# A new order for the first 441 of 973 steps of a gated linear attention kernel

## The chip, the core and the metric

The kernel runs on one core of a Trainium2 chip. That core has five engines, each with a queue of its own that it works off strictly in order: PE (TensorE, matrix products), DVE (VectorE), ACT (ScalarE), POOL (GpSimd) and SP (SyncE, which here only issues DMAs). They wait for each other through semaphores. The metric is the device time of one execution in microseconds (us), as the median of several runs.

## What is computed

Eight batches of eight heads, 576 tokens, 64 channels per head: a linear attention with a softmax of q over its channels and of k over the tokens, and after it a value product gated by a causal convolution of 5 taps, and an output product.

```python
q_s = softmax(q, axis=-1)            # over 64 channels
k_s = softmax(k, axis=2)             # over 576 tokens
kv  = einsum('bhsd,bhde->...', k_s^T v)      # 64x64 per head
x   = einsum('bhsd,bhde->bhse', q_s, kv)     # -> (8, 576, 512)
gate = sigmoid(sum_k conv_w[k] * shift(x, 4 - k))
out  = (gate * (x @ w_val)) @ w_out
```

The weights come as 64-bit floats and are put together on the chip into 32-bit ones.

## The kernel before

The work is cut into named steps; `ORDER` lists 973 of them as text ("`kv 1`", "`q_sub 0 2 p`"), and the program runs the list from top to bottom under a manual schedule. A step issues one or a few instructions on one engine, so the list sets the order of every engine's queue. A last letter names the engine where there is a choice: `a` ACT, `v` DVE, `p` POOL. The first number is the batch, the second mostly the part: channels lie across partitions, in four blocks of 128 (`x 1 0` is block 0 of batch 1). `HOMES` gives each tile the buffer that it takes, one digit per tile in order of allocation; a tile must wait until all readers of the buffer's last tenant are through. The four letters of `bank` are pairs of PSUM banks.

The steps that matter here:

- weights, eight slabs of 512 columns (0 to 3 are w_val, 4 to 7 w_out): `load_words`, then `part` and `field`, `scaled`, `signed`, `joined` make one 32-bit slab, `w_high` and `w_low` split it for two exact passes (L276 to L327). `value b m` needs slab m, `project b n` slab 4 + n, high and low both.
- q: `q_max`, `q_sub`, `q_exp` or `q_each`, `q_sum`, `q_eps`, `q_rec`, `q_mul` on five parts of the tokens (the fifth, the tail, is shared by two batches); `q_turn` transposes on PE, `q_turned` copies out, `tail_turn` and `tail_turned` do so for the tail.
- k of batches 0 and 1: `k_top`, `k_raise`, `k_turn`, `k_turned`, `k_tail_turn`, `k_tail_turned`. For later batches `k_peak` takes maxima per column, which go through memory (`k_row`, `k_spread`).
- `kv` (80 matmuls), `kv_sums` and `kv_norm` give `kvd`; `attend b 0` and `attend b 1` make x of blocks 0, 1 and 2, 3 in PSUM.
- x: `x_high` and `x_low` split x out of PSUM, `first` and four `tap` steps make the gate's sum from the same PSUM bank, `sigmoid` ends it. For batch 0, blocks 0 and 1, the convolution runs on PE as `conv` instead, which takes the banks of `x 0 0` and `x 0 1` as soon as `x_low` has read them.
- `value` (24 matmuls of 128x288, the products with the low part of x last, in the order in which `x_low` ran), `gated`, `g_high`, `g_low`, `project` (24 matmuls), `copy`, `put`.

`attend 1 1` takes the PSUM banks of `x 1 0` and of a projection; it cannot start before all four taps on `x 1 0` are through.

Of the kernel before, what the change touches and what calls it, by code (L numbers as in the profile page):

```python
# [31 lines left out]
    load_words 3, field 3 v, scaled 3 v, signed 3, w_high 3 a, warm 12, load_q 0 2 5, load_kc 0 0, load_q 0 0 1,  # L32
    load_taps, load_q 0 1 2, load_ident, load_words 0, part 3 a, load_kc 0 1, load_kc 0 2, load_kc 0 3, load_words 1,
    q_max 0 2 3, q_sub 0 2 p, q_max 0 3 5, joined 3 v, q_exp 0 2 3, k_top 0 0, q_sub 0 3 p, q_each 0 4, q_exp 0 3 4,
    q_max 0 0 1, q_each 0 0, tap_field p, tap_scaled v, load_v 0, load_vt 0, load_km 2 2, tap_part v, tap_signed,
    q_max 0 1 2, tap_joined p, diag p, load_km 2 1, load_words 2, load_q 1 0 5, q_sub 0 1 p, k_raise 0 0, q_sum 0 2 5,
    q_eps 0 2 5 p, q_exp 0 1 2, k_top 0 1, k_raise 0 1, k_turn 0 0, q_rec 0 2 5, field 0 p, k_top 0 2, k_raise 0 2,
    q_mul 0 2 p, k_top 0 3, k_raise 0 3, q_sum 0 0 2, q_eps 0 0 2 v, q_mul 0 3 p, q_rec 0 0 2, k_turn 0 1,
    k_turned 0 1 v, k_turned 0 0 a, k_tail_turn 0, k_tail_turned 0 v, scaled 0 a, field 1 p, scaled 1 a, signed 1,
    q_mul 0 1 a, q_mul 0 4 p, tail_turn 0, conv_rows, q_mul 0 0 p, part 1 a, load_kc 1 1, tail_turned 0 a, joined 1 p,  # L40
    field 2 p, scaled 2 p, signed 0, w_high 0 a, kv 0, k_peak 2 2, tail_high 0 a, kv_sums 0, kv_norm 0 v, part 2 a,
    conv_kv, signed 2, q_turn 0 0, q_turned 0 0 a, part 0 a, load_words 4, load_km 2 0, joined 0 p, q_turn 0 1,
    q_turned 0 1 a, attend 0 0, w_low 3 p, x_high 0 1 a, q_max 1 0 2, q_sub 1 1 p, x_low 0 1, x_high 0 0 a, x_low 0 0,
    load_words 5, attend 0 1, w_high 1 a, q_max 1 2 4, joined 2 p, x_high 0 3 a, first 0 3 a, tap 0 3 2, tap 0 3 3,
    tap 0 3 0, x_low 0 3, w_low 1 p, tap 0 3 1, load_words 6, first 0 2 a, q_exp 1 1 2, x_high 0 2 a, w_high 2 p,
    part 5 a, q_each 1 2, w_low 0 p, x_low 0 2, q_each 1 3, q_sub 1 0 p, load_kc 1 3, load_kc 1 0, k_top 1 1,
    k_top 1 0, k_top 1 3, tap 0 2 0, conv, field 5 p, scaled 5 p, signed 5, joined 5 p, load_v 1, field 4 p,
    conv_gate 1, conv_gate 0, load_kc 1 2, value 0 1, value 0 0, q_sum 1 2 4, k_raise 1 0, q_exp 1 0 1, k_raise 1 3,
    sigmoid 0 3, gated 0 1, w_low 2 p, k_top 1 2, gated 0 0, k_raise 1 1, k_raise 1 2, q_sum 1 0 2, load_km 2 3,
    scaled 4 p, signed 4, q_eps 1 2 4 p, q_rec 1 2 4, k_turn 1 0, k_turned 1 0 a, load_q 2 0 5, g_high 0 1 a,  # L50
# [5 lines left out]
    load_km 3 3, q_turned 1 1 a, gated 0 3, g_high 0 3 a, g_low 0 2 v, k_peak 3 2, attend 1 0, first 1 1 a, field 6 p,
    first 1 0 a, scaled 6 p, signed 6, tap 1 1 2, g_low 0 3 p, load_km 5 3, project 0 0, tap 1 0 3, load_k 2,
    tap 1 0 1, load_km 5 0, part 6 a, q_sub 2 1 p, w_high 6 a, k_row 2, x_high 1 1 a, project 0 1, tap 1 0 2,
    load_q 3 0 5, tap 1 1 3, q_sub 2 2 p, x_high 1 0 a, x_low 1 0, tap 1 0 0, k_spread 2, copy 0 0 a a, put 0 0,
    part 7 a, copy 0 1 a a, load_km 3 1, attend 1 1, x_high 1 3 a, first 1 2 a, k_peak 3 3, joined 6 p, load_qc 3 1,  # L60
    tap 1 1 1, x_high 1 2 a, signed 7, w_high 7 a, w_low 6 p, q_sub 2 4 p, tap 1 1 0, sigmoid 1 1, joined 7 p,
    x_low 1 1, q_sub 2 0 p, x_low 1 3, x_low 1 2, k_peak 3 1, load_kt 2, load_km 3 0, project 0 2, w_low 7 p,
    value 1 0, copy 0 2 a a, load_vt 4, k_peak 3 0, q_max 3 0 4, q_sub 2 3 p, put 0 2, first 1 3 a, tap 1 2 1,
    load_km 4 1, sigmoid 1 0, gated 1 0, k_sub 2 0 p, k_sub 2 2 p, tap 1 2 3, load_km 4 3, k_sub 2 4 p, q_sub 3 0 p,
    load_v 2, q_exp 2 0 5, q_sum 2 0 5, project 0 3, copy 0 3 a a, far 1 2 2, k_sub 2 1 p, k_sub 2 3 p, g_high 1 0 a,
    g_low 1 0 p, q_eps 2 0 5 a, q_rec 2 0 5, q_mul 2 0 p, q_mul 2 3 p, k_exp 2, k_row 3, kt_exp 2, q_mul 2 2 p,
    load_v 4, load_km 6 1, k_peak 4 3, k_peak 4 1, tap 1 2 0, tap 1 3 2, value 1 3, put 0 1, tap 1 3 3, tap 1 3 0,
    tap 1 3 1, value 1 1, gated 1 1, near 1 2 2, kv 2, kv_sums 2, load_km 4 0, kv_norm 2 v, q_mul 2 1 a, q_mul 2 4 a,
    q_turn 2 0, sigmoid 1 3, gated 1 3, k_peak 5 0, k_peak 5 3, sigmoid 1 2, tail_turn 2, q_turned 2 0 a,
    tail_turned 2 a, load_qc 3 0, tail_high 2 a, q_sub 3 1 v, q_sub 3 3 p, k_peak 4 0, put 0 3, k_spread 3,  # L70
    q_sub 3 2 p, g_high 1 3 p, g_low 1 3 v, g_high 1 1 p, g_low 1 1 v, q_turn 2 1, q_turned 2 1 a, load_q 4 0 5,
    value 1 2, gated 1 2, q_exp 3 0 4, attend 2 0, far 2 1 0, x_high 2 1 a, g_high 1 2 v, g_low 1 2 p, project 1 3,
    far 2 1 3, first 2 1 a, q_total 3, tap 2 1 1, load_km 4 2, first 2 0 a, tap 2 0 2, copy 1 3 a a, near 2 1 3,
    x_low 2 1, load_qc 3 3, tap 2 0 1, tap 2 1 2, tap 2 0 3, load_v 3, load_km 5 1, project 1 0, put 1 3, q_log 3,
    k_peak 4 2, k_sub 3 3 p, l_turn 3, near 2 1 0, l_row 3, far 2 0 0, k_row 4, q_max 4 0 5, k_sub 3 1 p,
    copy 1 0 a a, k_sub 3 0 p, load_km 5 2, project 1 2, copy 1 2 a a, k_sub 3 4 p, attend 2 1, first 2 3 a,
    x_high 2 0 a, near 2 0 0, first 2 2 a, project 1 1, x_high 2 3 a, q_sub 4 0 p, x_low 2 0, x_high 2 2 a, tap 2 3 1,
    k_sub 3 2 p, kt_exp 3, put 1 0, q_sub 4 2 p, copy 1 1 a a, sigmoid 2 0, q_sub 4 1 p, q_sub 4 4 p, k_peak 5 1,
    tap 2 2 0, sigmoid 2 1, l_spread 3, x_low 2 2, x_low 2 3, q_sub 4 3 p, tap 2 3 0, k_peak 6 1, value 2 1,
    gated 2 1, g_high 2 1 p, tail_high 3 a, l_sub 3 0 p, load_km 6 2, tap 2 2 1, q_exp 4 0 5, load_k 4, load_kt 4,  # L80
    tap 2 3 3, tap 2 2 2, k_exp 3, k_peak 6 2, tap 2 3 2, k_spread 4, c_exp 3 0, value 2 0, load_qc 3 2, l_sub 3 3 p,
    g_low 2 1 p, sigmoid 2 3, gated 2 0, load_qc 4 1, value 2 3, q_total 4, c_exp 3 3, gated 2 3, kv 3, value 2 2,
    kv_sums 3, load_q 5 0 5, k_peak 5 2, tap 2 2 3, kv_norm 3 v, l_sub 3 1 p, q_log 4, c_exp 3 1, attend 3 0,
    load_km 6 3, g_high 2 0 a, sigmoid 2 2, g_high 2 3 p, g_low 2 3 p, first 3 1 a, l_turn 4, gated 2 2, first 3 0 v,
    load_vt 6, far 3 1 0, k_row 5, tap 3 0 3, g_low 2 0 p, tap 3 0 1, g_high 2 2 p, put 1 1, g_low 2 2 p, project 2 0,
    x_high 3 1 v, l_sub 3 2 p, load_km 6 0, project 2 1, load_qc 4 3, tap 3 1 2, x_low 3 1, k_sub 4 3 p, put 1 2,
    c_exp 3 2, k_sub 4 4 p, copy 2 0 a a, tap 3 1 1, tap 3 1 3, x_high 3 0 a, l_row 4, copy 2 1 a a, q_max 5 0 4,
    k_sub 4 1 p, put 2 0, far 3 0 0, attend 3 1, load_qc 5 1, first 3 3 a, k_sub 4 2 p, first 3 2 a, q_sub 5 1 p,
    k_peak 6 3, x_high 3 3 a, put 2 1, k_sub 4 0 p, project 2 2, tap 3 0 2, q_sub 5 2 p, load_qc 4 0, l_spread 4,
    x_high 3 2 a, x_low 3 0, k_exp 4, x_low 3 3, tap 3 2 3, k_peak 6 0, project 2 3, copy 2 2 a v, near 3 0 0,  # L90
# [707 lines left out]
```

## Time and profile before

| | |
|---|---|
| time, median of 3 runs | 286.7 us (286.58 to 286.75) |
| profiled execution | 286.8 us, of which the span from first to last instruction is 284.9 us |
| PE busy | 278.9 us (98%) in 2640 matmuls |
| DVE busy | 232.0 us (81%) |
| POOL busy | 202.0 us (71%) |
| ACT busy | 193.1 us (68%) |
| granted TensorE clock | 1.00 of 2.4 GHz in all 40 slices |

Busy times are averages over the span; the first third is fuller than the last. A row of PE spans from the start of a matmul to its modelled end, and consecutive matmuls overlap, so PE counts as busy also where it runs below its rate. A row of DVE or POOL includes what it waited for after its start. Spans on POOL are rough.

### The profile page before, as it was taken

The page shows a single profiled execution, that of the slowest core. Times are in us where ns is not written, and L with a number is a line of the kernel's source. Part 1 is how long each engine was busy: PE and PEld are TensorE (multiplying, and loading weights), DVE is VectorE, ACT ScalarE, POOL GpSimd, SP SyncE. Part 2 cuts the span into 40 slices and gives each one's busy share as a digit, 9 for nine tenths or more (in the row PEclk, how much of TensorE's full clock was granted, in tenths as well). Part 3 has the DMA queues.
Part 4 walks back from the last instruction along what each step waited for, and adds up shares of the span by engine and source line. Part 5 has one row for each costly group of instructions (what it writes and reads, how often), then busy time and mean ns, then how long its engine had stood idle before and what let it go on. Part 6 is the DMA issues. An engine that isn't in the chain of part 4 may idle for free.

```text
span 284.9 us, 6648 instructions
## 1 busy us (share of the span) xinstructions
PE 278.9 (98%) x2640; PEld 250.5 (88%) x2640; DVE 232.0 (81%) x334; ACT 193.1 (68%) x323; POOL 202.0 (71%) x185
## 2 busy tenths in 40 slices
...
GB/s 224 391 413 400 410 378 204 189 208 238 333 221 412 39 238 327 315 248 210 382 412 254 206 246 336 268 157 138 158 163 156 222 0 2 44 41 85 0 83 85
DMA packets 23463, 62.93 MB, mean 221 GB/s; under 512 B 3432, under 2 KB 3976, under 8 KB 20744
## 3 DMA queue, kind: packets, MB, share of 16 engines
...
HBM read 52.96 MB, written 9.54 MB: 219 GB/s over the span
## 4 chain that ended last, share of the span: by engine, by line
PE 82%; ACT 6%; DVE 5%; POOL 3%; DMA 2%; issue 1%; SPq 0%; POOLq 0%
PE out_a L629 36%; PE val L629 32%; PE kv L520 6%; PE x L579 6%; DMA q<-in_q_tail 2%; DVE gate L604 1%; ACT q L505 1%; ACT qT L197 1%; POOL q L507 1%; PE qTps L545 1%; DVE ktop L375 1%; DVE qm L414 1%; POOL q L419 1%; DVE x L599 1%; ACT gh L197 1%
## 5 line engine op out<-in xcount | busy, mean ns | idle before, releaser
L629 PE MATMUL val<-x,w_val_hi 128*128 128x288 f32 x512 | 88.9, 295 | 0.0
L604 DVE SCALAR_TENSOR_TENSOR gate<-x,cw,gate 128x575 f32<-128x575 f32 (+3 forms) x98 | 78.3, 809 | 5.1 <-ACT gate L592 1.8
L629 PEld LDWEIGHTS val<-x,w_val_hi 128*128 128x128 f32 x512 | 75.2, 188 | 0.0
L629 PE MATMUL val<-x,w_val_lo 128*128 128x288 f32 x256 | 56.0, 300 | 0.0
L629 PE MATMUL out_a<-gh,w_out_lo 128*128 128x288 f32 x248 | 54.6, 301 | 0.0
L629 PE MATMUL out_a<-gh,w_out_hi 128*128 128x288 f32 x248 | 53.2, 296 | 0.0
L696 POOL TENSOR_TENSOR gl<-g,gh 128x576 fp32r<-128x576 f32 x22 | 32.2, 1465 | 17.9 <-DVE gh L199 8.3
L629 PEld LDWEIGHTS out_a<-gh,w_out_lo 128*128 128x128 f32 x248 | 39.3, 188 | 5.7 <-ACT o L203 1.8
L629 PE MATMUL out_a<-gl,w_out_hi 128*128 128x288 f32 x248 | 43.0, 295 | 0.0
L629 PEld LDWEIGHTS val<-x,w_val_lo 128*128 128x128 f32 x256 | 40.8, 188 | 1.3 <-DVE g L688 0.4
L613 POOL TENSOR_TENSOR gate<-gate,far 128x572 f32<-128x572 f32 (+3 forms) x22 | 29.1, 1325 | 17.6 <-DVE gate L604 9.7
L629 PEld LDWEIGHTS out_a<-gh,w_out_hi 128*128 128x128 f32 x248 | 39.8, 188 | 0.0
L203 ACT ACTIVATE o<-out_a 128x576 f32<-128x576 f32 x27 | 17.6, 651 | 31.7 <-PE out_a L629 29.8
L419 POOL TENSOR_TENSOR q<-q,qm 128x512 f32<-128x512 f32 x31 | 32.5, 1064 | 7.1 <-DVE qm L414 7.1
L629 PEld LDWEIGHTS out_a<-gl,w_out_hi 128*128 128x128 f32 x248 | 36.5, 189 | 0.0
L688 DVE SCALAR_TENSOR_TENSOR g<-gate,val 128x576 f32<-128x576 f32 x32 | 24.0, 749 | 14.0 <-PE val L629 8.2
L489 POOL TENSOR_TENSOR qc<-qc,lb 128x576 f32<-128x576 f32 (+1 forms) x17 | 24.2, 1432 | 9.7 <-DMA lb<-lrow 6.4
L354 POOL TENSOR_TENSOR k<-k,kmax 128x512 f32<-128x512 f32 x23 | 30.0, 1323 | 0.2
L599 DVE TENSOR_TENSOR x<-x,x 128x576 fp32r<-128x576 f32 x32 | 23.1, 749 | 2.5 <-ACT x L197 2.3
L616 ACT ACTIVATE gate<-gate 128x576 f32<-128x576 f32 x30 | 20.0, 683 | 7.5 <-DVE gate L604 7.3
L609 ACT ACTIVATE far<-x,cw 128x572 f32<-128x572 f32 (+3 forms) x22 | 16.2, 738 | 12.0 <-PE x L579 4.7
L197 ACT CAST x<-x 128x576 fp32r<-128x576 f32 x27 | 17.0, 642 | 7.1 <-PE x L579 4.3
(114 smaller groups left out, 457.3 us busy)
## 6 DMA issues: line engine op xcount, KB each, us to landing
...
```

Of the source, the lines that this page charges most:

```text
L197: nc.scalar.copy(out=out, in_=in_)
L203: nc.scalar.mul(out, in_, factor)
L354: engine(e).tensor_sub(kk[r, cs], kk[r, cs], mx[r, cs])
L419: engine(e).tensor_tensor(qq, qq, m, op=ALU.add if b < 2 else ALU.subtract)
L489: engine(e).tensor_sub(t, t, T["lb", b][:, p])
L599: nc.vector.tensor_sub(xl, T["x", b, p], T["xh", b, p].bitcast(F32))
L604: nc.vector.scalar_tensor_tensor(out=a, in0=x, scalar=w, in1=a, op0=ALU.mult, op1=ALU.add)
L613: nc.gpsimd.tensor_add(a, a, T["far", b, p, j])
L616: nc.scalar.activation(T["gate", b, p], T["gate", b, p], AF.Tanh, scale=0.5)
L629: nc.tensor.matmul(ps[:, cs], a[:, kb, ms], z[:, cs], start=(i == 0), stop=(i == len(parts) - 1))
L688: nc.vector.scalar_tensor_tensor(out=T["g", b, m], in0=T["gate", b, m], scalar=1.0, in1=T["val", b, m], op0=ALU.add, op1=ALU.mult)
L696: engine(e).tensor_sub(T["gl", b, m], T["g", b, m], T["gh", b, m].bitcast(F32))
```

## The change

The first 441 steps stand in a new order; the last 532 are as before. The same 973 steps are run. Of the first 441, 25 have another engine letter: from POOL to DVE `q_sub 0 2`, `q_mul 0 2`, `q_mul 0 0`, `q_eps 0 2 5`, `field 2`, `k_sub 3 1`; from DVE to POOL `joined 3`, `tap_scaled`, `q_sub 3 1`, `g_low 1 1`, `g_high 1 2`; from ACT to POOL `scaled 0`, `w_high 1`, `g_high 0 0`, `part 4`, `w_high 7`; from POOL to ACT `scaled 5`, `scaled 6`, `q_eps 1 2 4`, `g_high 1 3`, `g_high 2 1`; from DVE to ACT `q_eps 0 0 2`, `k_tail_turned 0`; from ACT to DVE `q_turned 2 0` and half of `copy 0 3`. The digits of `HOMES` follow the order. On PE, `tail_turn 0` moves ahead of the second `k_turn` of batch 0, and `q_turn 1 0` ahead of `kv 1`; `k_tail_turn 1` moves behind `value 0 3`. Two lines of the table, and some of the buffers:

```diff
-    q_max 2 0 5, q_mul 1 1 a, load_k 3, field 7 p, scaled 7 a, gated 0 2, g_high 0 2 a, kv 1, kv_sums 1, q_mul 1 2 p,
-    q_mul 1 0 p, q_turn 1 0, load_vt 2, w_low 4 p, tail_high 1 a, q_turned 1 0 a, kv_norm 1 v, q_turn 1 1,
...
+    q_mul 1 1 a, tap 0 2 3, sigmoid 0 2, q_turn 1 0, k_peak 3 2, k_peak 3 3, load_k 3, g_low 0 0 p, w_high 4 a,
...
+    k_peak 2 0, kv 1, kv_sums 1, kv_norm 1 v, load_v 2, joined 4 p, w_low 4 p, scaled 6 a, q_turned 1 0 a, q_turn 1 1,
...
-    "gate": "0123450123230154021345021354201534201532",
...
-    "f": "0123456103541206354036430214016032451036502104236540",
+    "f": "0123456103540156342104306240164502316504152653204135",
...
+    "gate": "0123450312203542130542310524130254130251",
```

Lines of the changed kernel's functions are one higher than before (L414 is L415).

On DVE at the start, from the sum over q's parts 2 to 4 (`qs`) to the norm of `kv 0`. Before:

```order
L429 TENSOR_REDUCE qs_187<-q_116 128x16
L438 TENSOR_SCALAR qs_187<-qs_187 128x16
L442 RECIPROCAL qs_187<-qs_187 128x16
L199 COPY k_223<-kps_1_214 128x4x256
L199 COPY ktz_83<-ktps_226 64x512
L290 TENSOR_SCALAR e_233<-e_233 128x512
L291 SCALAR_TENSOR_TENSOR e_233<-words_135,e_233 128x512
L290 TENSOR_SCALAR e_203<-e_203 128x512
L291 SCALAR_TENSOR_TENSOR e_203<-words_125,e_203 128x512
L339 TENSOR_REDUCE kpk_312<-km_2_170 128x1
L529 TENSOR_SCALAR ks_316<-kv_271 128x4
L530 RECIPROCAL ks_316<-ks_316 128x4
```

Now:

```order
L508 TENSOR_TENSOR q_99<-q_99,qs_167 128x512
L430 TENSOR_REDUCE qs_167<-q_99 128x16
L200 COPY k_230<-kps_1_215 128x4x256
L443 RECIPROCAL qs_167<-qs_167 128x16
L291 TENSOR_SCALAR e_203<-e_203 128x512
L292 SCALAR_TENSOR_TENSOR e_203<-words_114,e_203 128x512
L508 TENSOR_TENSOR q_99<-q_99,qs_167 128x512
L291 TENSOR_SCALAR e_225<-e_225 128x512
L292 SCALAR_TENSOR_TENSOR e_225<-words_136,e_225 128x512
L282 TENSOR_SCALAR e_304<-words_165 128x512
L340 TENSOR_REDUCE kpk_315<-km_2_161 128x1
L530 TENSOR_SCALAR ks_319<-kv_259 128x4
```

Two products with `qs` (L508) and `field 2` (L282) have come in, `ktz` (`k_tail_turned`) and the small sum ahead of the second reciprocal have gone; the other small sum (L439) has come from POOL.

On POOL, from q's products of batch 0 to the low parts of w_val (`f` is a joined slab, `e` one on its way). Before:

```order
L507 TENSOR_TENSOR q_116<-q_116,qs_187 128x512 x2
L281 TENSOR_SCALAR e_233<-words_135 128x512
L507 TENSOR_TENSOR q_116<-q_116,qs_187 128x512 x2
L294 TENSOR_TENSOR f_258<-e_233,f_258 128x512
L281 TENSOR_SCALAR e_265<-words_181 128x512
L205 TENSOR_SCALAR e_265<-e_265 128x512
L294 TENSOR_TENSOR f_336<-e_203,f_336 128x512
L327 TENSOR_TENSOR w_val_lo<-f_127,w_val_hi 128x4x128
L419 TENSOR_TENSOR q_183<-q_183,qm_366 128x512
L294 TENSOR_TENSOR f_321<-e_265,f_321 128x512
L327 TENSOR_TENSOR w_val_lo<-f_258,w_val_hi 128x4x128
L199 CAST w_val_hi<-e_265 128x4x128
```

Now:

```order
L200 CAST w_val_hi<-e_225 128x4x128
L206 TENSOR_SCALAR e_304<-e_304 128x512
L295 TENSOR_TENSOR f_325<-e_304,f_325 128x512
L328 TENSOR_TENSOR w_val_lo<-f_97,w_val_hi 128x4x128
L200 CAST w_val_hi<-e_304 128x4x128
L295 TENSOR_TENSOR f_356<-e_203,f_356 128x512
L420 TENSOR_TENSOR q_189<-q_189,qm_354 128x512
L295 TENSOR_TENSOR f_245<-e_225,f_245 128x512
L328 TENSOR_TENSOR w_val_lo<-f_245,w_val_hi 128x4x128
L420 TENSOR_TENSOR q_189<-q_189,qm_354 128x512
L282 TENSOR_SCALAR e_507<-words_393 128x512
L206 TENSOR_SCALAR f_516<-words_243 128x512
```

Three of four products have gone or moved, two `w_high` (CAST) and one `scaled` stand in; `field` of slab 5 and `part` of slab 4 (`words_393`, `f_516`) now come ahead of the `w_low 0` that follows.

On DVE behind `kv 1` (`ks`, `kvd`: its norm), to the taps on `x 1 0` (`x_0` there). Before:

```order
L536 TENSOR_TENSOR kvd_761<-kv_700,ks_741 128x256
L688 SCALAR_TENSOR_TENSOR g_3_775<-gate_3_390,val_3_654 128x576
L696 TENSOR_TENSOR gl_2_779<-g_2_696,gh_2_698 128x576
L339 TENSOR_REDUCE kpk_781<-km_2_652 128x1
L290 TENSOR_SCALAR e_795<-e_795 128x512
L291 SCALAR_TENSOR_TENSOR e_795<-words_398,e_795 128x512
L604 SCALAR_TENSOR_TENSOR gate_1_793<-x_1_784,cw,gate_1_793 128x574
L604 SCALAR_TENSOR_TENSOR gate_0_797<-x_0_783,cw,gate_0_797 128x575
L604 SCALAR_TENSOR_TENSOR gate_0_797<-x_0_783,cw,gate_0_797 128x573
L604 SCALAR_TENSOR_TENSOR gate_0_797<-x_0_783,cw,gate_0_797 128x574
L604 SCALAR_TENSOR_TENSOR gate_1_793<-x_1_784,cw,gate_1_793 128x575
L599 TENSOR_TENSOR x_1_0_876<-x_0_783,x_1_0_876 128x576
```

Now:

```order
L537 TENSOR_TENSOR kvd_764<-kv_720,ks_761 128x256
L291 TENSOR_SCALAR e_526<-e_526 128x512
L292 SCALAR_TENSOR_TENSOR e_526<-words_395,e_526 128x512
L697 TENSOR_TENSOR gl_2_818<-g_2_709,gh_2_715 128x576
L340 TENSOR_REDUCE kpk_315<-km_3_713 128x1
L340 TENSOR_REDUCE kpk_315<-km_1_163 128x1
L605 SCALAR_TENSOR_TENSOR gate_0_804<-x_0_785,cw,gate_0_804 128x575
L605 SCALAR_TENSOR_TENSOR gate_0_804<-x_0_785,cw,gate_0_804 128x572
L600 TENSOR_TENSOR x_1_0_813<-x_0_785,x_1_0_813 128x576
L605 SCALAR_TENSOR_TENSOR gate_0_804<-x_0_785,cw,gate_0_804 128x573
L605 SCALAR_TENSOR_TENSOR gate_1_859<-x_1_786,cw,gate_1_859 128x573
L605 SCALAR_TENSOR_TENSOR gate_0_804<-x_0_785,cw,gate_0_804 128x574
```

`gated 0 3` (L688) stands ahead of `kv 1` now; `signed 6` comes right behind the norm and `g_low 0 2` (L697) behind it; there are two `k_peak` instead of one; one `x_low` stands ahead of the last taps on `x_0`.

## Rows read from the trace of the kernel before

**Rows 1.** Waits of PE over the span: who for whom, total us, times, longest.
```profile
PE qTtps L559 <- POOL q L507: 0.8, 1, 0.8
```

**Rows 2.** Rows of the tile `cv` (conv), 26 to 34 us: waits by releaser, us, times.
```profile
  DVE x L599: 1.1, 2
```

**Rows 3.** Timeline of PE at conv and before `attend 1 0`: start, length, [idle <- releaser].
```profile
27.14 5.73 PE L675 MATMUL cv<-qT,dg 64*64 64x288 f32 x80
...
52.79 1.20 PE L579 MATMUL x<-qT,kvd 64*64 64x288 f32 x16 [0.24 <-ACT qT L197]
```

**Rows 4.** The chain that ended last, from 60 us: start, us, what.
```profile
60.59 1.13 PE x L579 x16
61.72 3.39 PE out_a L629 x24
```

**Rows 5.** Stretches: length; busy of PE, PEld, DVE, ACT, POOL; clock, DMA share, GB/s.
```profile
11.00:28.00 17.00, 15.35 (x174) 9.09 (x176) 16.30 (x26) 16.62 (x38) 13.95 (x16) 1.00 1.03 410
...
61.00:69.00 8.00, 8.00 (x67) 7.50 (x60) 7.97 (x12) 6.53 (x10) 6.73 (x7) 1.00 0.73 239
```

**Rows 6.** Timeline of DVE, start stretch, and one product at 83 us.
```profile
4.45 0.43 DVE L281 TENSOR_SCALAR e<-words 128x512 f32<-128x512 f32 x1 [4.45 <-DMA words<-in_w_val]
...
16.63 0.70 DVE L438 TENSOR_SCALAR qs<-qs 128x16 f32<-128x16 f32 x1
...
18.61 0.67 DVE L199 COPY ktz<-ktps 64x512 f32<-64x512 f32 x1
...
26.33 1.42 DVE L599 TENSOR_TENSOR x<-x,x 128x576 fp32r<-128x576 f32 x2
...
83.75 0.68 DVE L419 TENSOR_TENSOR q<-q,qm 128x512 f32<-128x512 f32 x1
```

**Rows 7.** Timeline of POOL, 27 to 34 us.
```profile
27.41 1.05 POOL L419 TENSOR_TENSOR q<-q,qm 128x512 f32<-128x512 f32 x1
28.41 1.30 POOL L294 TENSOR_TENSOR f<-e,f 128x512 int32<-128x512 int32 x1
29.65 1.30 POOL L327 TENSOR_TENSOR w_val_lo<-f,w_val_hi 128x512 fp32r<-128x512 f32 x1
...
33.84 0.65 POOL L281 TENSOR_SCALAR e<-words 128x512 f32<-128x512 f32 x1
```

**Rows 8.** Timeline of ACT at `q_turned 0 0`.
```profile
23.26 1.01 ACT L197 COPY qT<-qTps 128x1024 f32<-128x1024 f32 x1 [0.31 <-PE qTps L545]
```

**Rows 9.** Timeline of DVE around `kv 1` and batch 1.
```profile
49.63 0.74 DVE L688 SCALAR_TENSOR_TENSOR g<-gate,val 128x576 f32<-128x576 f32 x1
...
51.11 0.42 DVE L536 TENSOR_TENSOR kvd<-kv,ks 128x256 f32<-128x256 f32 x1
...
54.03 0.69 DVE L291 SCALAR_TENSOR_TENSOR e<-words,e 128x512 int32<-128x512 int32 x1
...
59.55 0.81 DVE L604 SCALAR_TENSOR_TENSOR gate<-x,cw,gate 128x572 f32<-128x572 f32 x1
...
63.44 2.07 DVE L599 TENSOR_TENSOR x<-x,x 128x576 fp32r<-128x576 f32 x3
```

**Rows 10.** Timeline of ACT, 50 to 53 us.
```profile
50.34 0.61 ACT L203 ACTIVATE e<-e 128x512 f32<-128x512 f32 x1
50.86 0.67 ACT L197 CAST gh<-g 128x576 fp32r<-128x576 f32 x1
...
51.73 1.92 ACT L197 COPY qT<-qTps 128x1024 f32<-128x1024 f32 x2
```

**Rows 11.** Timeline of POOL and DVE where both read two tensors at once.
```profile
54.30 1.73 POOL L696 TENSOR_TENSOR gl<-g,gh 128x576 fp32r<-128x576 f32 x1 [0.82 <-ACT gh L197]
...
264.03 1.44 POOL L696 TENSOR_TENSOR gl<-g,gh 128x576 fp32r<-128x576 f32 x1
...
264.11 1.97 DVE L696 TENSOR_TENSOR gl<-g,gh 128x576 fp32r<-128x576 f32 x1 [0.77 <-POOL gh L199]
...
267.73 0.76 DVE L696 TENSOR_TENSOR gl<-g,gh 128x576 fp32r<-128x576 f32 x1 [0.77 <-POOL gh L199]
```

235 lines of the change are left out of this document (118 added, 117 removed).

## The prediction

> **What bounds the kernel now.** I read the page's busy shares first: TensorE has matmuls nearly throughout (table above), so time can only be won where it waits. Then the waits of TensorE, of which the longest is 0.8 us for the product of q's tail, `tail_turn 0` [rows 1]. The rows of matmuls overlap, so short stalls hide under "busy"; one tile's rows show them: the instructions of `conv` waited 1.1 us for DVE's `x_low` [rows 2], inside the stretch from 27.14 to 32.87 [rows 3]. The wait before `attend 1 0` is 0.24 [rows 3]. All of these lie before 53 us. From 53 us on the chain of waits is TensorE alone [rows 4]: after `attend 1 0` at 52.79 come two projections, `attend 1 1` at 60.59 and a third projection to 65.1. So a gain has to come from the first 53 us, some 2 to 3 us at the very most (0.8 + 1.1 + 0.24 and a little), and every microsecond that TensorE is made to wait later is paid in full. Last I read how full the others are: from 11 to 28 us DVE works 16.30 of 17 us, from 61 to 69 us 7.97 of 8 [rows 5]. DVE is nearly as full as TensorE, so which instruction stands on DVE decides.
>
> **The start, to conv.** The diff moves steps between engines; I count the DVE queue up to `x_low 0 0`, on which conv waits. On it: three elementwise steps of 128x512 (`q_sub 0 2`, `q_mul 0 2`, `q_mul 0 0`), 0.68 each by DVE's one row of that form, `field 2` 0.43, `q_eps 0 2 5` 0.2 to 0.7 [rows 6]. Off it: `joined 3` (of the same size, 0.68 too), `q_eps 0 0 2` 0.70, `k_tail_turned 0` 0.67 [rows 6], `tap_scaled` (a few columns, some 0.2). On: 2.04 + 0.43 + 0.2 = 2.67; off: 2.25; net +0.42. Of DVE's 0.7 idle between 11 and 28 us [rows 5] I let 0.3 absorb it, the rest being short gaps between an instruction and the next that reads its result. That leaves +0.15. Then DVE and POOL get in each other's way: the `q_eps` of 0.70 us touches 16 columns only [rows 6], so most of it is a wait. The four moved instructions that read SBUF now meet POOL's queue (`q_eps 0 2 5` against `q_sub 0 1`, `q_mul 0 2` against `q_mul 0 4`); I take 0.2 for them together, nothing at the least, 1.05 (one whole POOL product, [rows 7]) at the most. `x_low 0 0` ended at 27.75 (26.33 + 1.42, [rows 6]); conv later by **+0.35**, bounds +0.1 and +1.2.
>
> The other way to conv is ACT: `q_exp 0 1 2` comes some 0.5 later, because on DVE one `q_max` more, some 0.6, stands ahead of `tap_signed`, for which POOL's `diag` and `q_sub 0 1` wait. ACT's own list up to `q_turned 0 0` is about as long as before (`scaled 0` goes, `k_tail_turned 0` and a small `q_eps` come), and ACT idled 0.31 there for the transposes [rows 8]; with `tail_turned 0` no longer waiting behind `signed`, I take this way as level, 0 to +0.3 and not added to DVE's +0.35, since the later of the two counts. `tail_turn 0` itself moves ahead of the second `k_turn`: its 0.8 us wait goes [rows 1], but what follows waits for ACT and DVE instead, so I count nothing for it.
>
> **POOL, to value 0 0.** POOL now does `w_high 1`, `joined 2`, `w_low 3`, `w_high 2`, `joined 0`, `q_sub 1 1`, `joined 1`, `w_low 1`, `q_sub 1 0`, `field 5`, `part 4`, `w_low 0`. `joined 2` waits for `signed 2` on DVE, which I put at 24.8 (it ended at 25.08 before, and now stands one `conv_kv` earlier but behind the longer queue). From there, start to start: five of joined and w_low at 1.24, two q_sub at 1.0 and 1.15, three with one input (`w_high 2`, `field 5`, `part 4`) at 0.6 to 0.7 [rows 7], together 10.3, and w_low 0's own 1.30: done at 36.4 to 36.5. `w_low 1` lies 3.9 earlier, 32.6, and is needed when conv ends, 32.87 before and 33.2 now: covered by 0.6. `w_low 0` is needed one product of 24 matmuls (3.2 to 3.3) later, at 36.4 to 36.5: **+0.1**, bounds 0 and +0.5 (`part 4` has no POOL row of its form).
>
> **kv 1 late.** `q_turn 1 0` now runs ahead of `kv 1`, so ACT can move its result while `kv 1` runs: the wait of 0.24 before `attend 1 0` goes [rows 3]. One more change of form on TensorE costs some 0.05. **-0.2**.
>
> **After kv 1.** Here lies the price. `attend 1 1` takes the PSUM bank of `x 1 0` and so waits for the last tap on it. Before, `kvd` was done at 51.53 and `attend 1 0` came 1.26 later (52.79), `attend 1 1` 7.8 after that [rows 3, 4, 9]: DVE had 9.06 us from kvd and needed 8.83 (59.55 + 0.81 - 51.53) [rows 9]. Now `attend 1 0` follows kvd at once: DVE has 7.9. Its list up to that tap (now `tap 1 0 2`) loses `gated 0 3`, one tap and the 0.20 wait and gains one `k_peak`: about -0.67 - 0.75 - 0.2 - 0.1 + 0.66, or 7.75. Spare 0.15. Nor is there room further on: the last `x_low` of batch 1 ended at 65.51 [rows 9], and `value 1 0`, which began at 65.1 (61.72 + 3.39, [rows 4]), reads it in its last group, 2.9 later: 2.5 spare. Now 1.2 of that is gone with kvd, and two `k_peak` and `tap 1 3 1` come in for `gated 0 3`, +1.4: nothing left.
>
> Into that queue falls a collision. Straight behind kvd stand the two-input instruction of `signed 6` and `g_low 0 2`, both with two SBUF inputs. kvd now ends at 51.53 + 0.98 (one `q_turn` more ahead of it) + 0.45 = 52.96, so they start at about 53.4 and 54.1. POOL's next is `g_low 0 3`, waiting for ACT's `g_high 0 3`. `gated 0 2` (49.63 before, [rows 9]) comes at 49.4: +0.45 from above, one `k_peak` of 0.66 less ahead. Behind its end at 50.15 ACT does g_high, scaled 6, q_turned, part 6, g_high: 0.57 + 0.52 + 0.95 + 0.57 + 0.67 = 3.3 (start to start, the last its whole length) [rows 10], ending at 53.45. So POOL's g_low asks at 53.5, in the middle of `signed 6`, and ahead of DVE's g_low. What that does is in the trace: a POOL g_low that met `signed 6` took 1.73 instead of 1.44, and a DVE g_low that met a POOL g_low took 1.97 instead of 0.76 [rows 9, 11]. So DVE's g_low waits out POOL's, 1.3 to 1.4 us; less the spare of 0.15, `attend 1 1` is **+1.2** late, bounds 0 and +1.4. Once paid it isn't paid again at `value 1 0`, since TensorE is later too.
>
> These rows are what the Trainium skill, "SBUF — State Buffer", section "Who interferes with whom", states as a rule: a DVE instruction with two SBUF inputs contends with a GpSimd instruction that reads SBUF, and the one that comes second blocks until the first is done. By that rule all three products moved to DVE are new collisions too, each up to one POOL product: the sum would then reach +1.2 at conv instead of +0.35, and 289.1 in all. I keep the smaller value, since the count puts POOL idle beside `q_mul 0 0` and the DVE one first beside `q_sub 0 2`.
>
> **Sum.** The profiled execution took 286.8 us: the span of 284.9 and 1.9 around it; it lies 0.1 over the median of 286.7. 0.35 + 0.1 - 0.2 + 1.2 = +1.45: 288.25 against 286.8, 288.2 against the median, if nothing later than 83 us is late. There the last 532 steps keep their order, and TensorE passes on what it got.
>
> **Rivals.** (a) No collision: ACT brings `g_high 0 3` after 54.1 and DVE's g_low goes first; 0.6 us decides, which is about what my count may be off. Then +0.25, 287.0, and up to 0.4 more at `value 1 0`, where nothing is spare. (b) The start gets shorter and the time falls: if the instructions on DVE up to `x_low 0 0` come without the collisions and the new order saves its waits, conv starts when `attend 0 1` is through, up to 1.1 us earlier [rows 2]; with the 0.2 at kv 1 and no loss later that is 286.7 - 0.2 - (0.5 to 1.1) = 285.4 to 286.0. For it: POOL is relieved of three products and two small sums by then, and all waits of TensorE lie there. Against it: DVE, the engine that conv waited for, gets more. It decides once `x_low 0 0` ends before 27.4 instead of 27.75. (c) A further late place: `q_turned 2 0` and half of `copy 0 3` come to DVE before 86 us (some 1.6), and the last `g_low` of batch 1 goes through POOL behind three more; where that outlasts TensorE, another 0.8 to 1.0: 289.2. That the table is not followed is no rival: the order of instructions is written out.
>
> **How the numbers follow.** Forecast (collision) 0.45, at 287.5 to 288.8; (a) 0.25; (b) 0.20; (c) 0.10. A run of this kernel can tell some 0.2% (0.57 us) from no change: faster is under 286.1, slower over 287.3. Faster 0.20 is (b); within 0.2%, 0.25, is (a); slower, 0.55, the forecast and (c). The range leaves out about half of (b) and most of (c): 285.7 to 288.9. The cases have both signs, and the forecast's own range is 287.5 to 288.8.
>
> **What would show it.** In the changed kernel's profile: `conv` begins its steady run at 28.1 (27.8 before); `value 0 0` begins at 36.5; no wait for ACT before `attend 1 0`, at 53.0; a DVE `gl` of about 2 us near 54 with a POOL `gl` beside it; `attend 1 1` at 62.0 instead of 60.8, with a wait for a DVE tap. Wrong would be: `conv` at or before 27.5 (then (b)), a `gl` of 0.76 on DVE near 54 (then (a)), or a wait of TensorE after 83 us (then (c)).

## The result: 1.0% slower, and more than half of it where no loss was forecast

The changed kernel takes 289.4 us (median of 4 runs, 289.05 to 290.0) against 286.6 us before: a ratio of 1.0098 (95% interval 1.0086 to 1.011), 2.7 us slower. That is the forecast sign, but outside the range: 288.2 was forecast, 288.9 was its upper end. The profiled execution has a span of 287.8 us (284.9 before), at a granted clock of 1.00.

TensorE's waits over the span, by who was waited for. Columns: total us, times, longest. Before the change the longest, behind the warm-up, was the 0.8 us for POOL's product [rows 1], and none lay behind 53 us.

```profile
PE kps L387 <- ACT kc L380: 1.1, 1, 1.1
PE x L580 <- ACT qT L198: 1.0, 2, 0.8
...
PE x L580 <- DVE gate L605: 0.9, 1, 0.9
PE out_a L630 <- POOL gl L697: 0.6, 1, 0.6
PE val L630 <- ACT x L198: 0.3, 1, 0.3
...
PE val L630 <- POOL w_val_lo L328: 0.2, 1, 0.2
```

The first two lie ahead of `conv`; the other four are new. To see what each is worth I took the start of each of TensorE's steps from the two timelines (the last column is rounded after subtracting):

| step | before | changed | later by |
|---|---|---|---|
| `conv` | 27.14 | 27.18 | 0.04 |
| `value 0 0` | 36.10 | 36.55 | 0.44 |
| `q_turn 1 1` | 51.52 | 51.89 | 0.37 |
| `attend 1 0` | 52.79 | 52.98 | 0.19 |
| `attend 1 1` | 60.52 | 61.67 | 1.14 |
| `kv 2` | 77.84 | 79.04 | 1.19 |
| `attend 2 0` | 85.96 | 87.05 | 1.08 |
| `project 1 0`, behind `project 1 3` | 90.39 | 92.30 | 1.91 |
| `project 1 1`, behind `attend 2 1` | 98.02 | 100.35 | 2.34 |
| `value 2 0`, behind `value 2 1` | 104.58 | 107.46 | 2.88 |

From there to the end the distance stays at 2.88. So there are five losses: 0.40 at `value 0 0`, 0.95 at `attend 1 1`, and, behind 83 us, 0.83, 0.43 and 0.54. The first two are those of the forecast, the last three are not.

**At 53 us** DVE and POOL, from their timelines (start, length):

```profile
53.20 0.69 DVE L292 SCALAR_TENSOR_TENSOR e<-words,e 128x512 int32<-128x512 int32 x1
53.82 1.98 DVE L697 TENSOR_TENSOR gl<-g,gh 128x576 fp32r<-128x576 f32 x1
```

```profile
53.65 1.53 POOL L697 TENSOR_TENSOR gl<-g,gh 128x576 fp32r<-128x576 f32 x1 [1.21 <-ACT gh L198]
```

POOL's `g_low 0 3` starts 0.17 us ahead of DVE's `g_low 0 2`, and DVE's takes 1.98 us; in [rows 11] an undisturbed one took 0.76. This is the forecast collision, within 0.3 us of where it was put. Before the change DVE's product ran first, and POOL's came at 54.30 [rows 11]:

```profile
52.11 0.89 DVE L696 TENSOR_TENSOR gl<-g,gh 128x576 fp32r<-128x576 f32 x1
```

**At 87 us** the same happens a second time:

```profile
86.29 0.74 DVE L340 TENSOR_REDUCE kpk<-km 128x1 f32<-128x576 f32 x1
86.95 1.82 DVE L697 TENSOR_TENSOR gl<-g,gh 128x576 fp32r<-128x576 f32 x1
88.90 0.75 DVE L689 SCALAR_TENSOR_TENSOR g<-gate,val 128x576 f32<-128x576 f32 x1
```

```profile
86.74 1.42 POOL L697 TENSOR_TENSOR gl<-g,gh 128x576 fp32r<-128x576 f32 x1
89.72 0.66 POOL L200 CAST gh<-g 128x576 fp32r<-128x576 f32 x1 [1.56 <-DVE g L689]
90.47 1.42 POOL L697 TENSOR_TENSOR gl<-g,gh 128x576 fp32r<-128x576 f32 x1
```

```profile
91.94 0.53 PE L630 MATMUL out_a<-gl,w_out_hi 128*128 128x288 f32 x2 [0.56 <-POOL gl L697]
```

DVE's `g_low 1 3` (86.95) meets POOL's `g_low 1 1`, which was on DVE before the change. There the two ran on DVE one after the other, 0.7 us each, and POOL stood idle:

```profile
85.02 1.41 DVE L696 TENSOR_TENSOR gl<-g,gh 128x576 fp32r<-128x576 f32 x2
```

```profile
87.74 1.43 POOL L696 TENSOR_TENSOR gl<-g,gh 128x576 fp32r<-128x576 f32 x1 [3.88 <-DVE gh L199]
```

In the changed kernel, behind the collision, `gated 1 2` (88.90), `g_high 1 2` and `g_low 1 2` come late one after the other, and `project 1 3` waits for the last.

**At 96 to 106 us** the queue of ACT, from its timeline:

```profile
96.66 1.28 ACT L617 ACT_TABLE_LOAD   x1
97.95 0.69 ACT L617 ACTIVATE gate<-gate 128x576 f32<-128x576 f32 x1
98.54 0.63 ACT L204 ACTIVATE o<-out_a 128x576 f32<-128x576 f32 x1
...
102.66 0.74 ACT L593 ACTIVATE gate<-x,cw 128x576 f32<-128x576 f32 x1
105.01 0.64 ACT L198 CAST x<-x 128x576 fp32r<-128x576 f32 x1 [1.60 <-DVE gate L605]
```

`sigmoid 2 0` (97.95) is the first function of its table behind the logarithm, so a table load of 1.28 us stands ahead of it, and `copy 1 0` (98.54), which frees a PSUM bank for the second half of `attend 2 1`, comes behind both. Then ACT stands idle 1.60 us ahead of `x_high 2 3` (105.01), for a tap on DVE, and `value 2 1` waits for `x_high 2 3`. Before the change `x_high 2 3`, the first of the two casts here, ran without a wait, and the load came behind it:

```profile
99.95 1.19 ACT L197 CAST x<-x 128x576 fp32r<-128x576 f32 x2
101.16 1.28 ACT L362 ACT_TABLE_LOAD   x1
```

### The profile page after: what moved, and what is told of

The parts are those of the page before. It is cut to its first block, busy times and chain, and to the rows that moved or that the text cites. A ratio compares the mean times of both kernels' runs of the same rounds, so it can differ in the third digit from the quotient of the medians.

```text
span 287.8 us, 6644 instructions
## 1 busy us (share of the span) xinstructions
PE 279.2 (97%) x2640; PEld 251.0 (87%) x2640; DVE 233.8 (81%) x335; ACT 192.1 (67%) x323; POOL 201.2 (70%) x184
## 4 chain that ended last, share of the span: by engine, by line
PE 68%; DVE 16%; DMA 5%; issue 4%; POOL 4%; ACT 2%; SPq 1%; DVEq 0%; POOLq 0%; ACTq 0%
PE val L630 30%; PE out_a L630 26%; PE kv L521 5%; DVE gate L605 5%; PE x L580 4%; DVE kpk L340 3%; DMA km<-in_k_strided 3%; DMA words<-in_w_val 2%; POOL w_val_lo L328 1%; DVE e L292 1%; DVE x L600 1%; DVE g L689 1%; POOL f L295 1%; DVE qs L449 1%; DVE gl L697 1%
## 5 line engine op out<-in xcount | busy, mean ns | idle before, releaser
L697 POOL TENSOR_TENSOR gl<-g,gh 128x576 fp32r<-128x576 f32 x23 | 32.9, 1435 | 15.5 <-ACT gh L198 8.3
L630 PEld LDWEIGHTS out_a<-gl,w_out_hi 128*128 128x128 f32 x248 | 36.4, 188 | 0.8 <-POOL gl L697 0.8
L204 ACT ACTIVATE o<-out_a 128x576 f32<-128x576 f32 x26 | 16.8, 647 | 29.2 <-PE out_a L630 27.3
L355 POOL TENSOR_TENSOR k<-k,kmax 128x512 f32<-128x512 f32 x22 | 28.8, 1326 | 0.2
```

What stands on the lines that cost most here:

```text
L204: nc.scalar.mul(out, in_, factor)
L355: engine(e).tensor_sub(kk[r, cs], kk[r, cs], mx[r, cs])
L630: nc.tensor.matmul(ps[:, cs], a[:, kb, ms], z[:, cs], start=(i == 0), stop=(i == len(parts) - 1))
L697: engine(e).tensor_sub(T["gl", b, m], T["g", b, m], T["gh", b, m].bitcast(F32))
```

## Experiments

Every kernel was run beside the kernel before; "ratio" is to that, with its 95% interval. Each edit is one of the order of steps, the buffers kept unless said (in e4 and e8 two digits of `bank` change places with two steps). The diffs show the list of steps with what does not matter left out.

The start of an execution varies (see "The start to conv" below), which hides small gains. So I also give the "way" in a run's one trace: the time from the start of `conv` to TensorE's last end. It is 254.59 us before the change and 257.43 in the changed kernel. How well it repeats shows in its first part, from `conv` to `value 0 0`: 9.34 to 9.37 us in the seven traces that have the changed list there (changed kernel, e1 to e6).

**e1: `g_low 0 2` ahead of `signed 6`**

```diff
-g_low 0 3 p, signed 6, joined 6 p, q_sub 2 1 p, g_low 0 2 v, field 7 p, k_peak 2 3, k_peak 2 1
+g_low 0 3 p, g_low 0 2 v, k_peak 2 3, k_peak 2 1, signed 6, joined 6 p, q_sub 2 1 p, field 7 p
```

> The changed kernel with g_low 0 2 taken ahead of signed 6 on DVE, and signed 6 (with joined 6, q_sub 2 1 and field 7 behind it on POOL) put behind the two k_peak that follow; the same instructions, in another order. Theory (the collision of two products that read two tensors each, on DVE and POOL, costs DVE 1.2 us): the row gl on DVE near 53 takes 0.75 us instead of 1.98, the last tap on x 1 0 ends 1.1 earlier, attend 1 1 starts at 60.8 to 61.0 instead of 61.67, the time falls from 289.4 to 288.4 to 288.7. Rival (gl takes long because it waits for its own input or its buffer): moved ahead by 1.1 us it ends at the same 55.8, attend 1 1 stays at 61.7 and the time at 289.4.

Measured: 288.4 us, ratio 1.0061 (1.0046 to 1.0076), 1.0 us under the changed kernel; way 256.41. DVE, then POOL:

```profile
52.50 0.75 DVE L697 TENSOR_TENSOR gl<-g,gh 128x576 fp32r<-128x576 f32 x1
```

```profile
53.39 1.42 POOL L697 TENSOR_TENSOR gl<-g,gh 128x576 fp32r<-128x576 f32 x1 [1.22 <-ACT gh L198]
```

The same instructions in another order, and `gl` takes 0.75. `attend 1 1` starts at 60.45, 33.55 behind `conv` (34.49 in the changed kernel). The rival falls: nothing that `gl` reads was late.

**e2: `g_low 1 3` ahead of `k_peak 5 1`**

```diff
-q_turned 2 0 v, k_peak 5 1, g_low 1 3 v
+q_turned 2 0 v, g_low 1 3 v, k_peak 5 1
```

> The changed kernel with k_peak 5 1 put behind g_low 1 3 on DVE instead of ahead of it: a swap of two neighbours. Theory (a second collision, with POOL's g_low 1 1 at 86.7, costs DVE 1.1 us and makes project 1 3 wait 0.83): gl on DVE starts at 86.3, before POOL's, takes 0.75 instead of 1.82; gated 1 2 comes at 87.7 instead of 88.9; project 1 3 runs without a gap of 0.86; the time falls from 289.4 to 288.5. Rival (project 1 3 waits because DVE's list is longer by q_turned 2 0, not because of the collision): the list is as long as before, gap and time stay, 289.4.

Measured: 288.5 us, ratio 1.0065 (1.0048 to 1.0082); way 256.32. DVE, then POOL:

```profile
85.85 0.98 DVE L697 TENSOR_TENSOR gl<-g,gh 128x576 fp32r<-128x576 f32 x1
86.75 0.74 DVE L340 TENSOR_REDUCE kpk<-km 128x1 f32<-128x576 f32 x1
87.41 0.74 DVE L689 SCALAR_TENSOR_TENSOR g<-gate,val 128x576 f32<-128x576 f32 x1
```

```profile
86.30 1.81 POOL L697 TENSOR_TENSOR gl<-g,gh 128x576 fp32r<-128x576 f32 x1
```

Now DVE is first, and POOL's product is the one that grows, from 1.42 to 1.81; POOL has room for it. DVE's list up to `gated 1 2` is as long as before, yet `gated 1 2` (87.41) starts 60.64 behind `conv` instead of 61.72, and the wait of `project 1 3` is gone: the collision set it, not the length.

**e3: both**, e1's and e2's diffs

> Both edits together, g_low 0 2 ahead of signed 6 and g_low 1 3 ahead of k_peak 5 1. Theory (two collisions, each paid in full at TensorE): the gains add, 0.9 + 0.8, the time is 287.6 to 287.9. Rival (what is won at attend 1 1 is lost again at a later wait, at attend 2 1 or value 2 1, since DVE is full): 288.4 or more.

Measured: 287.5 us (median of 10), ratio 1.0031 (1.0021 to 1.004); way 255.35. The gains add: 1.0 + 0.9 against 1.9.

**e4: `kv 1` first again**

```diff
-sigmoid 0 2, q_turn 1 0, k_peak 3 2, ... k_peak 2 0, kv 1, kv_sums 1
+sigmoid 0 2, k_peak 3 2, ... k_peak 2 0, kv 1, q_turn 1 0, kv_sums 1
```

> The changed kernel with q_turn 1 0 put back behind kv 1, as before the change; nothing else. Theory (the swap saves 0.24 us at attend 1 0 but takes 1 us from DVE between kvd and the last tap, and moves g_low 0 2 into POOL's g_low 0 3): kvd ends at 52.0 instead of 52.84, DVE's g_low starts ahead of POOL's and takes 0.75, attend 1 0 comes at 53.2 to 53.3 instead of 52.98, attend 1 1 at 60.9 to 61.2 instead of 61.67, the time is 288.6 to 289.0. Rival (the swap is a gain, the price lies elsewhere): attend 1 0 and all behind it come 0.24 later, 289.6.

Measured: 288.1 us, ratio 1.0051 (1.0036 to 1.0066), a larger gain than was expected; way 256.19. TensorE, DVE and POOL:

```profile
52.82 1.20 PE L580 MATMUL x<-qT,kvd 64*64 64x288 f32 x16 [0.23 <-ACT qT L198]
```

```profile
53.00 0.75 DVE L697 TENSOR_TENSOR gl<-g,gh 128x576 fp32r<-128x576 f32 x1
```

```profile
53.99 1.43 POOL L697 TENSOR_TENSOR gl<-g,gh 128x576 fp32r<-128x576 f32 x1 [1.92 <-ACT gh L198]
```

With `kv 1` first, DVE's product comes ahead of POOL's. The 0.23 us wait is back, and still `attend 1 1` comes 0.75 us earlier, counted from `conv` (33.73 behind it instead of 34.49): the swap saved 0.2 and cost 0.95 by moving DVE behind POOL. The rest of the gain over the expectation lies at 87 us, where DVE and POOL still collide but come earlier, and `project 1 3` loses 0.40 us instead of 0.83.

**e5: `copy 1 0` ahead of `sigmoid 2 0`**, on top of e3

```diff
-x_high 2 0 a, sigmoid 2 0, k_sub 3 4 p, ... copy 1 0 a a
+x_high 2 0 a, copy 1 0 a a, sigmoid 2 0, k_sub 3 4 p, ...
```

> The kernel of both DVE swaps (287.5) with copy 1 0 put ahead of sigmoid 2 0 on ACT. Theory (sigmoid 2 0 drags a table load of 1.28 us with it, and copy 1 0 behind it frees the bank of x 2 3 too late): the second half of attend 2 1 runs without its wait, 0.2 us off, 287.3; the wait of 0.55 at value 2 1 stays. Rival (attend 2 1 is late by DVE's x_low 2 0, which frees its first bank): no change, 287.5.

Measured: 287.25 us (9 runs), ratio 1.0022 (1.0013 to 1.0032), 0.24 under e3, which these intervals don't resolve. In its trace `project 1 1` starts 1.18 us behind the start of `attend 2 1` (1.56 in the changed kernel, 1.32 in e3, 1.14 before the change): half of this loss had gone with e2's swap. ACT:

```profile
94.33 0.67 ACT L204 ACTIVATE o<-out_a 128x576 f32<-128x576 f32 x1
95.01 1.28 ACT L617 ACT_TABLE_LOAD   x1
```

The same load is there; with the copy ahead of it, TensorE doesn't wait for the copy. But what is won there is lost one step on: `value 2 1` waits 0.45 us for `x_high 2 3` instead of 0.30, and the way is 255.37, as long as e3's. The time came out as the theory had it, yet the trace shows no gain by this edit alone.

**e6: `x_high 2 3` and two `x_low` ahead of the taps**, on top of e5

```diff
-q_max 4 0 5, first 2 3 a, tap 2 3 0, first 2 2 a, tap 2 2 2, tap 2 3 3, x_high 2 3 a, x_low 2 2, tap 2 2 1, x_low 2 3
+q_max 4 0 5, x_low 2 2, first 2 3 a, x_high 2 3 a, tap 2 3 0, x_low 2 3, first 2 2 a, tap 2 2 2, tap 2 3 3, tap 2 2 1
```

> As the run with copy 1 0 first, and x_high 2 3 put right behind first 2 3 on ACT, x_low 2 2 and x_low 2 3 ahead of the taps on x 2 2 and x 2 3 on DVE, as before the change. Theory (x_high 2 3 stands behind two DVE taps, since steps on one PSUM bank run one after another in the order of the list): value 2 1 runs without its gap of 0.58, the time is 286.6 to 286.8. Rival (ACT or DVE is simply full there): the gap moves to the last products of value 2 1 and the time stays at 287.3.

Measured: 286.7 us (11 runs), ratio 1.0007 (0.9998 to 1.0016), 0.5 under e5; way 254.91. ACT:

```profile
99.11 0.74 ACT L593 ACTIVATE gate<-x,cw 128x576 f32<-128x576 f32 x1
99.75 0.63 ACT L198 CAST x<-x 128x576 fp32r<-128x576 f32 x1
```

`x_high 2 3` follows `first 2 3` without the 1.60 us. It had waited for no data of that tap, only for its turn on the bank of `x 2 3`. The edit moves two `x_low` as well; but the waits of the changed kernel name ACT's `x`, so it was `x_high` that held TensorE.

**e7: `part 4` behind `w_low 0`**, on top of e6

```diff
-field 5 p, ... part 4 p, k_top 1 3, w_low 0 p
+field 5 p, ... k_top 1 3, w_low 0 p, part 4 p
```

> As the run before, and part 4 put behind w_low 0 on POOL, so that w_low 0 comes 0.73 earlier. Theory (value 0 0 waits for w_low 0, 0.35 to 0.4 us, the only loss that is left ahead of 53 us): value 0 0 begins when value 0 1 is through, the time falls by 0.35 to 286.3, at or below the kernel before (286.6). Rival (k_raise or k_turned of batch 1 holds TensorE next): no change, 286.7.

Measured: 286.6 us (11 runs), ratio 1.0003 (0.9994 to 1.0012); way 254.86. `value 0 0` starts without a wait (35.82), but the 0.4 us do not arrive: the waits of TensorE have one new row,

```profile
PE x L580 <- DVE gate L605: 0.3, 1, 0.3
```

at `attend 1 1`. Counted from `conv`, `attend 1 0` comes 0.49 us earlier than in e6 and `attend 1 1` only 0.12: the little spare that DVE had up to the last tap on `x 1 0` is used up.

**e8: `kv 1` first instead of e1's edit**, otherwise as e7

```diff
-g_low 0 2 v, k_peak 2 3, k_peak 2 1, signed 6, joined 6 p, q_sub 2 1 p, field 7 p
+signed 6, joined 6 p, q_sub 2 1 p, g_low 0 2 v, field 7 p, k_peak 2 3, k_peak 2 1
...
-sigmoid 0 2, q_turn 1 0, k_peak 3 2, ... kv 1, kv_sums 1
+sigmoid 0 2, k_peak 3 2, ... kv 1, q_turn 1 0, kv_sums 1
```

> As the run before, but with kv 1 ahead of q_turn 1 0 in place of the swap at signed 6. Theory (kv 1 first gives up the 0.24 us at attend 1 0 and takes DVE out of POOL's way at 53 without any other edit): 0.2 slower than the run before, 286.5. Rival (the two ways are worth the same or more): 286.3 or less.

Measured: 286.5 us (11 runs), ratio 0.9999 (0.9991 to 1.0008): no difference from e7 that these runs resolve, nor from the kernel before. The way is 254.55, 0.31 shorter than e7's, which speaks for the rival; it is level with the 254.59 of the kernel before.

**e9: two more places**, on top of e7

```diff
-first 1 1 a, tap 1 1 1, ... tap 1 0 2, copy 0 1 a a
+first 1 1 a, tap 1 0 2, tap 1 1 1, ... copy 0 1 a a
...
-sigmoid 2 1, l_spread 3, project 1 1, copy 1 1 a a
+l_spread 3, project 1 1, copy 1 1 a a, sigmoid 2 1
```

> The kernel with the two DVE swaps, copy 1 0, x_high 2 3 and w_low 0 mended (286.6), with tap 1 0 2 ahead of tap 1 1 1 on DVE and copy 1 1 ahead of sigmoid 2 1 on ACT. Theory (what w_low 0 won is lost at attend 1 1, which waits 0.3 us for tap 1 0 2, since DVE has no spare between kvd and that tap; value 2 0 waits 0.15 for copy 1 1): attend 1 1 comes right after project 0 0, 0.35 earlier, the time is 286.1 to 286.3, under the kernel before (286.6). Rival (DVE is as late at value 1 0 or behind it): 286.6.

Measured: 286.75 us (11 runs), ratio 1.0005 (0.9996 to 1.0014): the rival; way 254.87, e7's length. (Its trace is of the slowest of the eleven, 287.6; what made that one slow lies ahead of `conv`, which starts at 27.65.) `attend 1 1` does come 0.37 us earlier, counted from `conv`, but the last ten products of `value 1 0`, which read the `x_low` of batch 1, take 1.84 us (1.50 before the change):

```profile
67.14 1.84 PE L630 MATMUL val<-x,w_val_hi 128*128 128x288 f32 x10
```

**e13: `k_peak 3 0` behind `x_low 1 2`**, on top of e9

```diff
-k_peak 3 0, x_low 1 3, x_low 1 2, tap 1 3 0
+x_low 1 3, x_low 1 2, k_peak 3 0, tap 1 3 0
```

> As the run with tap 1 0 2 first (286.7, where value 1 0 waited 0.35 us in its last products), and k_peak 3 0 put behind x_low 1 2 on DVE. Theory (DVE has no spare up to x_low 1 2, so what was won at attend 1 1 was lost at value 1 0): value 1 0 runs without that gap, 286.2 to 286.4, under the kernel before (286.6). Rival (the next full place takes it again): 286.6.

Measured: 286.8 us (12 runs), ratio 1.0002 (0.9992 to 1.0012): the rival again; way 254.87. At `value 1 0` the theory holds,

```profile
66.42 1.50 PE L630 MATMUL val<-x,w_val_hi 128*128 128x288 f32 x10
```

but, against the kernel before, time is lost in smaller pieces behind it: 0.25 us at the transposes of batch 2, whose q comes from POOL, and 0.15 us at `project 2 2`.

**e11: two products back on POOL**, in the changed kernel

```diff
-q_mul 0 2 v, ... q_mul 0 0 v
+q_mul 0 2 p, ... q_mul 0 0 p
```

> The changed kernel with q_mul 0 2 and q_mul 0 0 back on POOL, as before the change, in the same places of the list. The prediction's step: two products less on DVE, 1.36 us, bring x_low 0 0 and conv 0.35 us forward, 289.0. Theory now (ACT's chain of q_turned and x_high sets x_low 0 0, DVE only just keeps up): conv starts within 0.2 of the changed kernel, the time stays at 289.2 to 289.6, unless POOL's longer list delays w_low 0 and value 0 0 further.

Measured: 289.9 us, ratio 1.0117 (1.0103 to 1.0131): 0.5 us slower than the changed kernel, about as much as these intervals resolve. Neither expectation holds; the sign of the prediction's step is wrong. DVE, then POOL, then ACT's `q_exp 0 1 2`:

```profile
19.05 1.26 DVE L291 TENSOR_SCALAR e<-e 128x512 int32<-128x512 int32 x1 [0.28 <-POOL e L206]
```

```profile
18.98 1.04 POOL L508 TENSOR_TENSOR q<-q,qs 128x512 f32<-128x512 f32 x1
```

```profile
14.03 0.61 ACT L424 ACTIVATE q<-q 128x512 f32<-128x512 f32 x1
```

With `q_mul 0 0` on POOL, the first instruction of `signed 0` on DVE takes 1.26 us; in the changed kernel it is this row:

```profile
19.06 0.36 DVE L291 TENSOR_SCALAR e<-e 128x512 int32<-128x512 int32 x1
```

Through `dg`, for which `attend 0 1` then waits, this reaches `conv`, at 27.47. That is 13.44 us behind `q_exp 0 1 2`, where the changed kernel has 12.80 (27.18 against 14.38): 0.64 later. So on POOL the product makes a collision; on DVE there is none.

**e10: the tail's product back**, in the changed kernel, with other banks

```diff
-q_mul 0 4 p, tail_turn 0, ... k_turn 0 1, ... tail_turned 0 a, ... k_tail_turn 0, k_turned 0 0 a
+q_mul 0 4 p, ... k_turn 0 1, ... k_tail_turn 0, tail_turn 0, k_turned 0 0 a, tail_turned 0 a
...
-    "bank": ("0123023103120...
+    "bank": ("0130231023120...
```

> The changed kernel with tail_turn 0 back behind k_tail_turn 0, and tail_turned 0 behind k_turned 0 0 on ACT (banks of batch 0 changed to match), as before the change. Theory (TensorE waits 0.8 us for ACT's q_turned 0 0 ahead of attend 0 0, so the place of the tail's product does not set the start of conv): conv_rows comes 0.6 to 0.8 later, attend 0 0 and conv within 0.2 of the changed kernel, the time 289.2 to 289.6. Rival (the early tail is worth the 0.8 us wait that it removed): 290.0 or more.

Measured: 290.4 us, ratio 1.0136 (1.0122 to 1.015), 1.0 us slower than the changed kernel. It doesn't tell the two apart, since the banks that I chose made a wait of their own, in the waits of TensorE:

```profile
PE x L580 <- DVE dg L661: 1.6, 1, 1.6
```

**e12: the same with better banks**

```diff
-    "bank": ("0123023103120...
+    "bank": ("3103201323120...
```

> As the run with the tail's product back, but with banks such that attend 0 0 takes none whose last reader is DVE's dg (there it waited 1.6 us for dg); attend 0 1 takes it, as in the changed kernel. Theory (the loss of 1.0 in that run was the bank): attend 0 0 waits for ACT's q_turned 0 0 as in the changed kernel, 289.2 to 289.7. Rival (the early tail itself is worth 0.5 to 1.0, since on ACT tail_turned 0 then stands between k_turned 0 0 and q_turned 0 0 and waits): conv 0.5 or more later, 289.9 or more.

Measured: 289.8 us, ratio 1.0109 (1.0085 to 1.0134), 0.4 us slower than the changed kernel, which these intervals don't resolve; way 257.13. `conv` starts at 27.59. ACT:

```profile
14.01 0.61 ACT L424 ACTIVATE q<-q 128x512 f32<-128x512 f32 x1
...
18.24 0.59 ACT L198 COPY qTt<-qTtps 128x512 f32<-128x512 f32 x1 [0.72 <-PE qTtps L560]
```

ACT stands idle 0.72 us for the tail's product, in the queue that leads to `q_turned 0 0`, and `conv` starts 13.58 us behind `q_exp 0 1 2` instead of 12.80. So at `conv` the early tail is worth 0.8 us. Of that 0.3 comes back, as `value 0 0` no longer waits for `w_low 0` and the way is that much shorter; 0.5 are left, near the measured 0.4. The rest of e10's loss, 0.6, came with its banks.

## Why the prediction was wrong

It put the time at 288.2 by four terms up to 65 us and nothing behind them. Up to `kv 2` its sum was +1.45; measured is +1.19. Behind that it has 0; measured is +1.69. By its own steps:

- **"... if nothing later than 83 us is late. There the last 532 steps keep their order ..."** This is the step that failed. Some 90 of the 441 reordered steps run behind 83 us, up to `tap 2 3 1` at 109 us on DVE, and the sum put them at nothing. There lie a collision of the very kind that the prediction costed at 53 us (0.83; e2), a copy behind a table load (0.43; half of it goes with e2's swap, and with the copy moved ahead, e5, TensorE loses the rest one step later) and an `x_high` behind two taps (0.54; e6). The rival (c) had the place in part, but as more work on DVE, `q_turned 2 0` and half of `copy 0 3`, and on POOL, at 0.8 to 1.0 us and with a chance of 0.10. With those instructions left where the change put them, e2 took the first loss away. That its 289.2 lies near the measured 289.4 is luck.
- **The start to conv, +0.35.** Too much: `conv` came 0.04 later. `x_low 0 0` ended at 27.79 (26.38 + 1.41) against 27.75. DVE's queue did grow, by 0.46 of busy time where +0.42 was counted, but its idle time took it in, as the stretch from 11 to 28 us shows (DVE is the third pair; 16.30 in [rows 5]):

```profile
11.00:28.00 17.00, 14.48 (x174) 9.04 (x176) 16.76 (x31) 16.30 (x38) 11.41 (x14) 1.00 1.03 408
```

  The later of the two ways was the other one, over ACT, which the prediction put level. Its first instruction is `q_exp 0 1 2`; here it is before the change, then in the changed kernel, and then DVE's maxima ahead of it in the changed kernel:

```profile
13.82 0.61 ACT L423 ACTIVATE q<-q 128x512 f32<-128x512 f32 x1
```

```profile
14.38 0.63 ACT L424 ACTIVATE q<-q 128x512 f32<-128x512 f32 x1 [0.45 <-POOL q L420]
```

```profile
9.17 1.49 DVE L415 TENSOR_REDUCE qm<-q 128x8 f32<-128x512 f32 x2 [0.31 <-DMA q<-in_q]
```

  `conv` starts 12.79 to 12.82 us behind `q_exp 0 1 2` in all eleven traces that have the changed list up to there (the changed kernel, e1 to e9, e13), and 13.32 before the change: ACT's way is 0.5 us shorter. But `q_exp 0 1 2` comes later, as was forecast ("some 0.5"), by 0.56 in this trace, since it waits for POOL's `q_sub 0 1`. How much later differs from execution to execution: it starts at 13.97 to 14.85 in the eleven traces, and `conv` with it at 26.77 to 27.65. The trace with the latest, e9's, has DVE waiting 0.71 and 0.18 us for DMAs of q there; the one with the earliest, e2's, has no such wait. Of the kernel before there is one trace.

  What the prediction feared, collisions by the products on DVE, is what they avoid: the three took 0.68, 0.74 and 0.68 us there, and with two of them back on POOL `conv` came 0.64 later (e11). "I count nothing" for the early tail was too low as well; it is worth 0.8 at `conv` and some 0.5 in the end (e12).
- **POOL, to value 0 0.** `w_low 0` ended at 36.49 (35.20 + 1.29), in the forecast 36.4 to 36.5. Since `conv` was not late, all of it shows as lost time: 0.40 instead of 0.1. The two errors cancel, and that the sum of these steps, +0.45, was met with +0.44 is luck.
- **kv 1 late, -0.2.** Right: 0.18 (from 0.37 to 0.19 later), and `attend 1 0` at 52.98 with no wait for ACT.
- **After kv 1, +1.2.** Right in place, in partners and in which one waits; 0.95 in size: the collision cost DVE 1.23 (1.98 against e1's 0.75), and its spare was 0.28, not 0.15. e1 and e4 take the collision away by two different edits, and the loss goes with it.
- **"Once paid it isn't paid again at value 1 0."** Right: 0.04.

By their medians the mends lead back from 289.4 to 286.6, the time before: 1.9 (e3), 0.24 (e5), 0.52 (e6) and 0.09 (e7). The ways say which of these are gains: 257.43 in the changed kernel, 255.35 in e3, 255.37 in e5, 254.91 in e6, 254.86 in e7, and 254.59 before the change. No version here beats both kernels: e8, the fastest, can't be told from the kernel before. What the new order gains at one place is taken up by the next full place each time (`attend 1 1` in e7, `value 1 0` in e9, batch 2 in e13).

These collisions are what the Trainium skill, "SBUF — State Buffer", section "Who interferes with whom", describes, and the runs bear out more of it than the prediction used: issue order decides who blocks (DVE 1.98 us behind POOL in the changed kernel, POOL 1.81 behind DVE in e2). It also names `tensor_scalar`, with one input, as able to contend (1.26 us in e11), and says that `tensor_reduce` never does: in e13 two `kpk` beside a POOL `gl` took 1.41 us together, 0.75 each at most, which is what one took with POOL idle (84.35 in the kernel before).

```profile
52.70 1.41 DVE L340 TENSOR_REDUCE kpk<-km 128x1 f32<-128x576 f32 x2
```

```profile
53.32 1.43 POOL L697 TENSOR_TENSOR gl<-g,gh 128x576 fp32r<-128x576 f32 x1 [1.22 <-ACT gh L198]
```
